# Grouping the eight PV tiles of a step by row half, in a fused attention and gated-MLP kernel

**The chip, the cores and the metric.** The kernel runs on one core of a Trainium2 chip. The metric is the device time of one execution in microseconds (us), as the median of several. All runs of the kernel before and of the change were of the fast state. A single run of a kernel has no state; where only one was made, the text says so.

## The reference, cut to what matters

`x` is 2048 tokens of 576 features. One branch is causal attention with a window of 256 and 32 heads of 18 features, the other a gated MLP; the output joins the two.

```python
q, k, v = split_heads(layernorm(x) @ wqkv)           # 32 heads, 18 features each
scores = jnp.einsum("bhqd,bhkd->bhqk", q, k) * (Dh ** -0.5)
scores = jnp.where(causal_window_256, scores, -1e9)
p = _softmax(scores, axis=-1)
o = jnp.einsum("bhqk,bhkd->bhqd", p, v)              # the PV product: the change is here
s = merge_heads(o) @ wo
g = _silu(_B_ref(layernorm(x), w_gate, w_up, w_down))    # 576 -> 4608 -> 576
return x + s * g
```

## The kernel before

Tokens are worked on in four chunks of 512. A scheduler in the program orders all work at build time from estimated durations; the matmuls of attention are set between those of the MLP. A "PV call" multiplies the exponentials of eight heads (`expr`, keys on the partitions) with their values (`v_aug`, 18 features and a column of ones, so 19 columns). It is a sequence of steps, one per block of 64 keys. In each step the program uses TensorE as eight tiles of 64 rows and 32 columns: two row halves (`i`), for the two halves of the partitions, by four column positions (`g`, `t`). Each tile loads its own 64x19 weights and streams its own columns, which are the queries that can see this block of keys: 64 to 320 of them.

```python
PV_ORDER = (0, 5, -4, -3, -2, -1, 1, 2, 3, 4, 6, 7)
...
ROWS = (slice(0, 64), slice(64, 128))
...
        kss = [ks for ks in PV_ORDER if c or ks >= 0]
        span = {ks: (max(ks, 0), min(ks + 5, SPC)) for ks in kss}

        def f_pv(eng):
            res = None
            outs = self.halves(hp, NT)
            for n, ks in enumerate(kss):
                q0, q1 = span[ks]
                cols = slice(q0 * SW, q1 * SW)
                for g, (hg, where, _) in enumerate(pend):
                    se = where[(ks, q0)]
                    ...
                    for t in range(2):
                        o = sub_pos(c, ks) * VSZ + (2 * hg + t) * VH
                        p0 = 32 * (2 * g + t)
                        for i in range(2):
                            res = eng.matmul(outs[i][p0:p0 + VH, cols], self.v_aug[ROWS[i], o:o + VH],
                                             self.expr[ROWS[i], se, t, cols], start=n == 0, stop=n == len(kss) - 1,
                                             tile_position=(64 * i, p0), skip_group_check=True)
            return res
```

`outs[0]` and `outs[1]` are two neighbouring blocks of 512 columns of the PSUM tensor `ps`, one for each row half. The first chunk has no keys before it, so its four calls have 8 steps (64 matmuls); the other twelve calls have 12 (96 matmuls), of 320, 192, 64, 128, 192, 256, 320, 320, 320, 256, 128 and 64 columns.

Of the kernel before, what the change touches and what calls it, by code (L numbers as in the profile page):

```python
# [32 lines left out]
VH = DH + 1  # L33
VSZ = (H // 2) * VH
# [58 lines left out]
def mm_ns(n):  # L93
    return max(24.7, n / 2.4 + 2.7)
# [9 lines left out]
def unit_slot(c, u):  # L104
    if u < 0:
        return 2 if c % 2 == 0 else 1
    return 0 if u == 0 else (1 if c % 2 == 0 else 2)


def sub_pos(c, ks):  # L110
    return unit_slot(c, ks // 4) * 4 + ks % 4
# [21 lines left out]
def dve_ns(n, rate=1.0):  # L133
    return n / (0.96 * rate) + 160.0
# [114 lines left out]
class Builder:  # L249
# [17 lines left out]
    def op(self, eng, est, fn, name="", deps=(), prio=3, nbytes=0, odeps=(), acq=None):  # L267
        o = Op(eng, est, fn, name, deps, prio, nbytes, odeps, acq)
        o.cidx = len(self.ops)
        self.ops.append(o)  # L270
        for d in o.deps:
            d.succs.append(o)
        for d in o.odeps:
            d.succs.append(o)
        return o
# [502 lines left out]
    def build_pv(self, c, pr):  # L778
        op = self.op
        pend, self.pend = self.pend, []  # L780
        hp = self.pool_s.hold()
        k0 = c * BPC
        vdeps = [self.op_v[kb] for kb in range(max(0, k0 - 2), k0 + BPC)]
# [6 lines that stand above are left out]
            for n, ks in enumerate(kss):  # L790
                q0, q1 = span[ks]
                cols = slice(q0 * SW, q1 * SW)
                for g, (hg, where, _) in enumerate(pend):
                    se = where[(ks, q0)]
                    assert all(where[(ks, q)] == se for q in range(q0, q1))
                    for t in range(2):
                        o = sub_pos(c, ks) * VSZ + (2 * hg + t) * VH
                        p0 = 32 * (2 * g + t)
                        for i in range(2):
                            res = eng.matmul(outs[i][p0:p0 + VH, cols], self.v_aug[ROWS[i], o:o + VH],  # L800
                                             self.expr[ROWS[i], se, t, cols], start=n == 0, stop=n == len(kss) - 1,
                                             tile_position=(64 * i, p0), skip_group_check=True)
            return res
        est = TURN_NS + sum(mm_ns((b - a) * SW) for a, b in span.values())
        pv = op("PE", est, f_pv, f"pv:{c}:{pr}", deps=[[m for _, _, rd in pend for m, _ in rd], vdeps], prio=1, acq=hp)
        for hg, _, rd in pend:
            self.op_pv[(c, hg)] = pv
            for se in sorted({se for _, se in rd}):
                self.r_ex.release(se, pv)
        for i in range(2):  # L810
            p1, d1 = self.r_ot1.produce()
            p2, d2 = self.r_o2.produce()
            p3, d3 = self.r_o2T.produce()
            o1 = self.ot1[:, p1, :].rearrange("p (b d) -> p b d", d=32)
            o2 = self.o2[:, p2, :].rearrange("p (b d) -> p b d", d=32)

            def f_t1(e, i=i, p1=p1):
                return e.transpose(self.ot1[:, p1, :], self.halves(hp, NT)[i])  # L818
            t1 = op("DVE", dve_ns(NT), f_t1, f"ot:{c}:{pr}:{i}", deps=[pv, d1], prio=1)
            hp.release(t1)  # L820
            rc = op("DVE", 255, lambda e, o1=o1: e.reciprocal(o1[:, :, DH], o1[:, :, DH]), f"rc:{c}:{pr}:{i}", deps=[t1], prio=1)
            on = op("DVE", dve_ns(NT // 32 * DH), lambda e, o1=o1, o2=o2: e.tensor_tensor(
                o2[:, :, 0:DH], o1[:, :, 0:DH], o1[:, :, DH:VH].broadcast_to([P, NT // 32, DH]), ALU.mult),
                f"on:{c}:{pr}:{i}", deps=[rc, d2, self.op_o2z], prio=1)
            self.r_ot1.release(p1, on)
            t2 = op("DVE", dve_ns(NT), lambda e, p2=p2, p3=p3: e.transpose(self.o2T[:, p3, :], self.o2[:, p2, :]),  # L826
                    f"ot2:{c}:{pr}:{i}", deps=[on, d3], prio=1)
            self.r_o2.release(p2, t2)
            for n, (k, r0, j0, i0, ni) in enumerate(self.o_moves(pr, i)):
                dst = self.oT[r0:r0 + ni, k, :]  # L830
                sr = self.o2T[32 * j0 + i0:32 * j0 + i0 + ni, p3, :]
                o = self.dma(dst, sr, ni * NT * 2, f"dma:o:{c}:{pr}:{i}:{n}", ("o", pr, i), deps=[t2, self.wo_last], prio=1, eng=OENG[i])
                o.slack = 1000.0
                self.r_o2T.release(p3, o)
                self.op_o.setdefault(c, []).append(o)
        if pr == 0:
            self.op_o[c].append(op("DVE", dve_ns(NT, 4.0), lambda e: e.tensor_copy(self.oT[ROWS[1], 0, :], self.oT[ROWS[0], 0, :]), f"odup:{c}",
                                   deps=[self.op_o[c], self.wo_last], prio=1))
# [458 lines left out]
```

## Time and profile before

| | |
|---|---|
| time, median of the first 3 runs | 560.82 us (560.54 to 561.11) |
| span of the profiled run, granted clock | 558.9 us, 1.000 |
| TensorE (PE) busy | 99% of the span |
| PV calls | 16, 1408 matmuls |

The prediction below shows the totals, the chain and the edges of a call. Here are three of the PV groups, by width of the moving operand. The columns are: line, engine, operation, output and inputs, stationary shape and moving shape, count; then busy time in us and the mean ns of one; then the idle time before them.

```profile
L800 PE MATMUL ps<-expr,v_aug 64*19 64x320 bf16 x512 | 14.7, 297 | 0.0
...
L800 PE MATMUL ps<-expr,v_aug 64*19 64x128 bf16 x224 | 7.2, 216 | 0.0
...
L800 PE MATMUL ps<-expr,v_aug 64*19 64x64 bf16 x224 | 6.4, 189 | 0.0
```

The 512 widest matmuls take 297 ns each, which would be 152 us one after another, but they keep TensorE busy for only 14.7 us: about ten of these records, tails included, lie over each other at a time. So the mean duration says little of the cost. It contains a tail (a 64-column matmul has 189 ns, but in the trace the next step follows a 64-column step after 29 ns) that lies under the next matmuls. What costs is the interval from one step to the next.

### The profile page before, as it was taken

To read this page: it belongs to the slowest core of one execution; us is meant where nothing else is said; L and a number is where in the kernel's file an instruction comes from. 1 tells how busy PE (TensorE), PEld (TensorE's weight loads), DVE (VectorE), ACT (ScalarE), POOL (GpSimd) and SP (SyncE) were. 2 spreads that over 40 slices of the span, in tenths; PEclk is the share of its full clock that TensorE was granted. 3 is DMA by queue.
4 is the path that set the end of the run, shared out by engine and by line. 5 is a ranking of instruction groups with operands and counts; after the bars stand their busy time and mean duration, and the time that the engine had idled before them with its cause. 6 is when DMAs were issued, how large, how long until landed. Compare 5 with 4: busy or idle time off the path is not lost.

```text
span 558.9 us, 19273 instructions
## 1 busy us (share of the span) xinstructions
PE 553.0 (99%) x8342; PEld 339.5 (61%) x8342; DVE 333.6 (60%) x797; ACT 274.3 (49%) x383; POOL 210.8 (38%) x360
## 2 busy tenths in 40 slices
PE   8999999999999999999999999999999999999996
PEld 7454444677755545467886555545688754444786
DVE  5477788687568767574558757357567623333033
ACT  4245654443657655645656464565756342323011
POOL 5564456566245444440667534035373200000000
PEclk9999999999999999999999999999999999999999
DMA  8988997831125534435121264244501035551010
GB/s 224 311 239 191 218 270 221 204 51 45 54 71 155 161 110 144 139 112 95 28 62 44 78 196 115 84 134 130 166 24 47 20 110 154 160 171 48 2 45 23
DMA packets 113468, 67.83 MB, mean 121 GB/s; under 512 B 18620, under 2 KB 111516, under 8 KB 113384
## 3 DMA queue, kind: packets, MB, share of 16 engines
q1 hardware_dynamic: 105960, 60.68, 39.8%
q0 software_dynamic: 7424, 5.92, 4.0%
q8 instruction: 66, 1.08, 0.8%
q14 instruction: 18, 0.15, 0.1%
HBM read 55.15 MB, written 2.36 MB: 103 GB/s over the span
## 4 chain that ended last, share of the span: by engine, by line
PE 98%; DVE 1%; DMA 0%; issue 0%; DVEq 0%
PE ps L121 94%; PE ps L800 3%; DMA x<-in_A_x_dram 0%; DVE small L524 0%; DVE small L526 0%; PE ps L598 0%; DVE xnr L540 0%; DVE s_attn L1061 0%; DVE thf L1066 0%; DVE xnr L544 0%; DVE small L528 0%; DVE small L530 0%; DVE xf L1071 0%; DVEq L1226 0%
## 5 line engine op out<-in xcount | busy, mean ns | idle before, releaser
L121 PE MATMUL ps<-xnT,wgs 64*128 64x512 bf16 (+1 forms) x2400 | 282.5, 368 | 0.1
L750 ACT ACTIVATE expr<-ps 128x1024 bf16<-128x1024 f32 (+4 forms) x160 | 154.9, 969 | 77.8 <-PE ps L121 77.2
L121 PEld LDWEIGHTS ps<-xnT,wgs 64*128 64x128 bf16 x2400 | 113.9, 94 | 114.8 <-DVE hT L948 1.6
L121 PE MATMUL ps<-wd_sb,hT 64*128 64x288 bf16 (+2 forms) x2448 | 156.7, 276 | 0.0
L948 DVE SCALAR_TENSOR_TENSOR hT<-tring,ps 128x512 bf16<-128x512 bf16 x144 | 98.3, 683 | 94.5 <-ACT tring L945 93.4
L945 ACT ACTIVATE tring<-ps 128x512 bf16<-128x512 f32 x144 | 86.1, 598 | 129.7 <-PE ps L121 127.5
L121 PEld LDWEIGHTS ps<-wd_sb,hT 64*128 64x128 bf16 x2448 | 112.4, 94 | 28.6
L278 POOL DMA_DIRECT2D qk<-qd x160 | 82.5, 522 | 119.4 <-PE ps L121 109.5
L763 DVE TENSOR_TENSOR expr<-expr,mask 128x128 bf16<-128x128 bf16 (+2 forms) x240 | 63.6, 298 | 62.0 <-ACT expr L750 61.5
L714 POOL TENSOR_SCALAR kx<-kprev,small 128x256 bf16<-128x256 bf16 x64 | 61.4, 969 | 28.1 <-PE ps L121 27.4
L121 PE MATMUL ps<-qk,kx 64*128 64x320 bf16 (+1 forms) x704 | 59.4, 254 | 0.0
L278 POOL DMA_DIRECT2D oT<-o2T x72 | 36.5, 514 | 58.5 <-DVE o2T L826 49.6
L121 PE MATMUL ps<-xnT,wgr 64*128 64x512 bf16 (+1 forms) x300 | 55.9, 367 | 0.0
L121 PEld LDWEIGHTS ps<-qk,kx 64*128 64x128 bf16 x704 | 31.2, 94 | 21.5 <-ACT expr L750 0.5
L121 PE MATMUL ps<-xnT,wqk 64*128 64x512 bf16 x256 | 32.6, 376 | 0.0
L1051 ACT ACTIVATE thf<-ps 128x576 bf16<-128x576 f32 (+3 forms) x22 | 11.4, 519 | 39.7 <-PE ps L121 39.4
L818 DVE STREAM_TRANSPOSE ot<-ps 128x512 f32<-128x512 f32 x32 | 22.4, 700 | 11.6 <-PE ps L800 11.5
L714 DVE TENSOR_SCALAR kx<-qk,small 128x512 bf16<-128x512 bf16 x64 | 22.4, 378 | 4.7 <-PE ps L121 4.1
L121 PEld LDWEIGHTS ps<-xnT,wgr 64*128 64x128 bf16 x300 | 14.9, 94 | 16.5
L826 DVE STREAM_TRANSPOSE o2T<-o 128x512 bf16<-128x512 bf16 x32 | 22.7, 711 | 1.0
L636 DVE CAST qd<-ps 128x1024 bf16<-128x1024 f32 (+1 forms) x20 | 22.1, 1110 | 1.5 <-PE ps L121 1.5
L696 ACT ACTIVATE v_aug<-ps 64x288 bf16<-64x288 f32 x32 | 13.1, 409 | 17.3 <-PE ps L121 16.8
(71 smaller groups left out, 302.1 us busy)
## 6 DMA issues: line engine op xcount, KB each, us to landing
wgs<-in_B_w_gate_dram SPq DMA_DIRECT2D x72, 256.0 KB, 3.3
wgs<-in_B_w_up_dram SPq DMA_DIRECT2D x72, 256.0 KB, 3.7
wd_sb<-in_B_w_down_dram SPq DMA_DIRECT2D x9, 576.0 KB, 6.3
qk<-qd POOLq DMA_DIRECT2D x100, 36.0 KB, 2.7
wgr<-in_B_w_gate_dram SPq DMA_DIRECT2D x36, 64.0 KB, 2.2
wgr<-in_B_w_up_dram SPq DMA_DIRECT2D x36, 64.0 KB, 2.5
xf<-in_A_x_dram SPq DMA_DIRECT2D x16, 144.0 KB, 2.6
out_dram<-xf SPq DMA_DIRECT2D x15, 144.0 KB, 1.8
```

Of the source, the lines that this page charges most:

```text
L121: res = eng.matmul(outs[i], lhs(ROWS[t], i), rhs(ROWS[t], i), start=start, stop=stop, tile_position=(64 * t, 0))
L278: o = self.op(eng, DMA_ISSUE_NS[eng], lambda e: e.dma_start(dst, src), name, deps, prio, nbytes=nbytes)
L636: return eng.tensor_copy(dst, self.both(h, n))
L696: return eng.activation(dst, src, ACTF.Copy)
L714: return e.tensor_scalar(self.kx[:, sx, pos:pos + n_ // SW, t, :], src.rearrange("p (s k) -> p s k", k=SW), self.half[:, t:t + 1], None, A ...
L750: return eng.activation(self.expr[:, se, :, lo * SW:NT], self.both(h, NT)[:, :, lo * SW:NT], ACTF.Exp, scale=SM_SCALE)
L763: return eng.tensor_tensor(e_, e_, m_, ALU.mult)
L800: res = eng.matmul(outs[i][p0:p0 + VH, cols], self.v_aug[ROWS[i], o:o + VH], self.expr[ROWS[i], se, t, cols], start=n == 0, stop=n == len( ...
L818: return e.transpose(self.ot1[:, p1, :], self.halves(hp, NT)[i])
L826: t2 = op("DVE", dve_ns(NT), lambda e, p2=p2, p3=p3: e.transpose(self.o2T[:, p3, :], self.o2[:, p2, :]), f"ot2:{c}:{pr}:{i}", deps=[on, d3 ...
L945: th = op("ACT", act_ns(NT), lambda e: e.activation(self.tring[:, st, :], bank(h, 0), ACTF.Tanh, scale=0.5), f"th:{c}:{ft}", deps=[pg, dt_ ...
L948: mu = op("DVE", dve_ns(NT), lambda e: e.scalar_tensor_tensor(self.hT[:, ft, :], self.tring[:, st, :], 1.0, bank(h, 1), ALU.add, ALU.mult) ...
```

## The change

The intent is to issue the four tiles of the upper row half together and then those of the lower half, where the kernel before alternates between the halves. The loop over `i` moves from the innermost place to the outermost within a step; operands, flags, counts and the order of steps stay.

```diff
-                for g, (hg, where, _) in enumerate(pend):
-                    se = where[(ks, q0)]
-                    assert all(where[(ks, q)] == se for q in range(q0, q1))
-                    for t in range(2):
-                        o = sub_pos(c, ks) * VSZ + (2 * hg + t) * VH
-                        p0 = 32 * (2 * g + t)
-                        for i in range(2):
+                for i in range(2):
+                    for g, (hg, where, _) in enumerate(pend):
+                        se = where[(ks, q0)]
+                        assert all(where[(ks, q)] == se for q in range(q0, q1))
+                        for t in range(2):
+                            o = sub_pos(c, ks) * VSZ + (2 * hg + t) * VH
+                            p0 = 32 * (2 * g + t)
                             res = eng.matmul(outs[i][p0:p0 + VH, cols], self.v_aug[ROWS[i], o:o + VH],
```

Passages are cut from the recorded text, at the marks, since no trace or run here shows what they rest on: one paragraph, two estimates of a call's length in term 1, and what was said in favour of rival (a), except that an alternating order was chosen here. The sum stands without them: 0 for terms 1, 3 and 4, and 0.1 us slower for term 2 (0.3 if neighbours in one half cost 3 ns each, a supposition): 560.82 + 0.1 = 560.9 us. By "streaming interval" understand what the steps of the first chunk show: 56, 83, 109 and 136 ns after 128, 192, 256 and 320 columns, so some 27 ns for every 64 columns. That steps follow "exactly" at it holds for these, not after the first step of a call (141 to 142 ns) nor after the fourth of a long one (76 ns after 128 columns).

> **What bounds the kernel now.** I read the totals and the chain of waits first, since a reordering inside TensorE's program can only matter if TensorE sets the end.
>
> ```profile
> PE 553.0 (99%) x8342; PEld 339.5 (61%) x8342; DVE 333.6 (60%) x797; ACT 274.3 (49%) x383; POOL 210.8 (38%) x360
> ...
> PE 98%; DVE 1%; DMA 0%; issue 0%; DVEq 0%
> PE ps L121 94%; PE ps L800 3%; DMA x<-in_A_x_dram 0%; DVE small L524 0%; DVE small L526 0%; PE ps L598 0%; DVE xnr L540 0%; DVE s_attn L1061 0%; DVE thf L1066 0%; DVE xnr L544 0%; DVE small L528 0%; DVE small L530 0%; DVE xf L1071 0%; DVEq L1226 0%
> ```
>
> The reader is to see that TensorE (PE) is busy 99% of the span and holds 98% of the chain, and that the changed line, L800 (the PV matmuls), has 3% of it: 3% of 558.9 us is some 19 us. Whatever a PV step gains or loses goes into the end almost one to one, but there are only 19 us to work on.
>
> The chain in order of time shows how those 19 us are made up:
>
> ```profile
> 63.72 0.94 PE ps L800 x64
> ...
> 129.41 0.94 PE ps L800 x64
> 130.35 33.52 PE ps L121 x496
> 163.87 1.27 PE ps L800 x90
> ...
> 438.92 1.27 PE ps L800 x89
> ```
>
> There are sixteen PV calls: four of 64 matmuls (first chunk, 8 steps) at 0.94 us, twelve of 96 (12 steps; a few records are merged into the neighbouring piece) at 1.27 us. 4 x 0.94 + 12 x 1.27 = 19.0 us.
>
> Next I ask what sets the time inside one call: the array, or the issue. The view of line L800 and the stretches of the call that starts at 163.80 us (columns: busy time and instructions in flight of the matmuls, then of the weight loads; the clock; the DMA share and rate):
>
> ```profile
> L800 PEld LDWEIGHTS ps<-expr,v_aug x1408: 83/88/90, 63.7 to 439.9; 64*19 64x19 bf16 x176
> L800 PE MATMUL ps<-expr,v_aug x1408: 189/269/303, 63.7 to 440.0; 64*19 64x320 bf16 x64, 64*19 64x128 bf16 x40, 64*19 64x192 bf16 x28, 64*19 64x256 bf16 x28
> ...
> 163.80:163.93 0.13, 0.13 (x8) 0.13 (x16) 1.00 1.01 300
> 163.95:164.02 0.07, 0.07 (x16) 0.07 (x8) 1.00 1.95 476
> ```
>
> The first stretch is the first step (320 columns): all eight tiles are in flight together, four of the upper row half and four of the lower, and sixteen weight loads (this step's and the next's) have been issued in the same 130 ns. In the trace's single records the eight matmuls of this step start at 0, 4, 7, 10, 14, 17, 20 and 24 ns, and the next step starts 142 ns after the first. In the first chunk the steps start at 0, 141, 224, 360, 495, 631, 740 and 796 ns: the intervals after a 320-column step are 136, 135, 136, after 256 columns 109, after 192 columns 83, after 128 columns 56 ns. So eight tiles take the time of one column stream, and the call is bounded by the array's streaming at full clock, not by the order in which tiles are handed over.
>
> The edges of a call:
>
> ```profile
> 163.49 0.38 PE L121 MATMUL ps<-xnT,wgr 64*128 64x512 bf16 x2
> 163.80 1.34 PE L800 MATMUL ps<-expr,v_aug 64*19 64x320 bf16 x96
> 165.07 0.40 PE L121 MATMUL ps<-qk,kx 64*128 64x64 bf16 x6
> ```
>
> By the single records the next work's first weight load starts 117 to 118 ns after the **last** PV matmul's start (64470 + 4 to 64591 in one call, 164953 to 165071 in another), whichever half it needs, and its loads for both halves go out 3 ns apart.
>
> [...]
>
> **The change part by part.** It removes and adds no instruction: 1408 PV matmuls and as many loads before and after, with the same operands, banks, start and stop flags. It moves them: a step's order goes from U0 L0 U1 L1 U2 L2 U3 L3 to U0 U1 U2 U3 L0 L1 L2 L3. Every tile still comes once in eight, so each tile's next matmul still waits for its own previous one a full step earlier. Term by term:
> 1. Streaming: the sum of the steps per tile is 30 x 64 columns = 1920 in the first chunk and 40 x 64 = 2560 later. [...] Order does not enter. Change: 0.
> 2. Spread within a step: 24 ns in the first chunk (3.3 ns per matmul), 55 ns at the end of the longer calls (last step's last matmul at 1154 against 1099 at its sorted start; by then loads and matmuls arrive about every 4.1 ns each, so a pair in 8.3 ns and eight pairs in 66 ns, longer than the 29 or 56 ns of a 64- or 128-column step). This is supply of instructions, the same number in any order. Change: 0, unless two neighbours in one half cost more than two in different halves; if they cost 3 ns more each, six such neighbours a step add 18 ns once per call as a spread that stays, 16 x 18 = 0.3 us.
> 3. The edge to the next work: it waits for the last matmul, which is L3 both before and after. Change: 0. The upper half is done some 3 positions earlier (3 x 8 = 24 ns), but nothing starts half an array earlier in the trace; if it did, 16 x 24 ns = 0.4 us would be gained.
> 4. Other engines: the PV result's semaphore is set by the same last matmul, so the transposes after it start as before; the order of all other work is computed from estimates the change leaves alone.
> Sum: 0, give or take 0.4 us; I lean 0.1 us to slower for term 2.
>
> **The rivals.** (a) Grouping serialises the loads or matmuls of one half[...]. If two of the four loads of 88 ns a step became visible, 176 steps (4 x 8 + 12 x 12) would add 176 x 176 ns = 31 us, 5.5% slower; one visible load per step 15 us, 2.8%. [...] Against it: the alternating order already has a same-half matmul in flight under every load, and steps follow at exactly the streaming interval. I give it 1%. (b) Alternation itself costs, so fewer changes of half (2 a step in place of 8) speed up PV: at most the 30 ns of extra spread in each of the twelve long calls, 0.4 us, since steps already run at the streaming interval. It can't reach 2%, which would be 11 us of 19. (c) The PV time changes but is hidden by a wait: the chain holds TensorE nearly throughout, so nothing would hide it; this only says that a real difference would be seen.
>
> **Range and chances.** 560.82 + 0.1 gives 560.9 us. The runs before lie within 0.3 us of their median; with 0.4 us for terms 2 and 3 either way and a little for another session, the range is 559.9 to 562.0. Two per cent is 11.2 us, more than half of all PV time, so within 2%: 0.985; slower 0.01 for rival (a), faster 0.005.
>
> **What would show it right or wrong.** In the changed profile: PV calls in the chain of 0.94 and 1.27 us again; eight matmuls in flight in a call's first 130 ns; step intervals of 136 ns after 320 columns; the next work 117 ns after the last PV start. Rival (a) would show as step intervals well over 136 ns or fewer than eight tiles in flight; rival (b) as calls shorter by up to 0.03 us; early start of one half as an edge under 100 ns. The prediction fails if a conflict exists between tiles of one half that only their being neighbours in the program brings out.

## The result, and the profile after

| | before | after |
|---|---|---|
| median of 6 runs | 560.92 us (560.54 to 561.15) | 560.88 us (560.45 to 561.7) |
| ratio after to before | | 1.0, 95% interval 0.9987 to 1.0013 |
| span of the profiled run, granted clock | 558.9 us, 1.000 | 559.3 us, 0.998 |

A ratio is the mean time of one kernel's fast runs over that of the other's of the same rounds, so it is not quite the ratio of the medians. The time is the same.

The totals and the PV calls in the chain of the changed kernel:

```profile
PE 552.5 (99%) x8342; PEld 338.6 (61%) x8342; DVE 333.5 (60%) x797; ACT 274.4 (49%) x383; POOL 210.7 (38%) x360
...
64.16 0.94 PE ps L800 x64
...
129.85 0.94 PE ps L800 x64
...
164.31 1.27 PE ps L800 x89
...
439.35 1.27 PE ps L800 x90
```

Every call takes the 0.94 or 1.27 us that it took before. The first PV call starts at 64.16 us, where it started at 63.72: the 0.4 us by which this one profiled span is longer arose before the first instruction that the change touches, and is no effect of it. From the first call's start to the last one's it is 375.19 us (439.35 - 64.16), against 375.20 before (438.92 - 63.72).

The same two stretches of a call as in the prediction (matmuls busy and in flight, weight loads busy and in flight, clock, DMA), and the edges of the call:

```profile
164.24:164.37 0.13, 0.13 (x8) 0.13 (x16) 1.00 1.13 331
164.39:164.46 0.07, 0.07 (x16) 0.07 (x8) 1.00 0.87 256
```

```profile
163.93 0.38 PE L121 MATMUL ps<-xnT,wgr 64*128 64x512 bf16 x2
164.24 1.34 PE L800 MATMUL ps<-expr,v_aug 64*19 64x320 bf16 x96
165.51 0.40 PE L121 MATMUL ps<-qk,kx 64*128 64x64 bf16 x6
```

Again eight matmuls and sixteen loads in the first 130 ns, a busy 1.34 us, and 1.27 us from the call's start to the next work. By the single records, the steps of this call start at 0, 142, 225, 253, 329, 411, 520, 655, 790, 925, 1034 and 1090 ns (a step's first matmul, told by its width). In the kernel before, the call of the same place has 0, 142, 224, 253, 329, 411, 519, 654, 789, 925, 1034 and 1090. Inside a step, starts are shifted by 4 ns at most (all calls, one by one among the matmuls of a width). Nothing was gained and paid back elsewhere: the changed calls are the same.

### The profile page after: what moved, and what is told of

Read it like the earlier page. It is cut to its first block, busy times and chain, and to the rows that moved or that the text cites. A ratio compares the mean times of both kernels' runs of the same rounds, so it can differ in the third digit from the quotient of the medians.

```text
span 559.3 us, 19273 instructions
## 1 busy us (share of the span) xinstructions
PE 552.5 (99%) x8342; PEld 338.6 (61%) x8342; DVE 333.5 (60%) x797; ACT 274.4 (49%) x383; POOL 210.7 (38%) x360
## 4 chain that ended last, share of the span: by engine, by line
PE 98%; DVE 1%; DMA 0%; issue 0%; DVEq 0%
PE ps L121 94%; PE ps L800 3%; DMA x<-in_A_x_dram 0%; DVE small L524 0%; DVE small L526 0%; PE ps L598 0%; DVE xnr L540 0%; DVE s_attn L1061 0%; DVE thf L1066 0%; DVE xnr L544 0%; DVE small L528 0%; DVE small L530 0%; DVE xf L1071 0%; DVEq L1226 0%
## 5 line engine op out<-in xcount | busy, mean ns | idle before, releaser
L696 ACT ACTIVATE v_aug<-ps 64x288 bf16<-64x288 f32 x32 | 13.1, 409 | 17.3 <-PE ps L121 16.8
```

The costliest lines, as they stand in the source:

```text
L696: return eng.activation(dst, src, ACTF.Copy)
```

## The experiments

That a call did not change doesn't say why. The prediction argued that each tile still comes once in eight, so each waits only for a matmul a full step back. That carries a picture of how TensorE hands out work, which is the author's assumption, and the experiments test it. ("Pair" below is a weight load with its matmul; a single record holds shape and time, not the tile, so a matmul is told by its width.) **Theory A**: matmuls start strictly in program order, each waiting for the earlier one on its own tile. Rivals: order is free, or free within limits, because matmuls wait in queues; or neighbours in one half do cost, but something hid it.

For most of the runs the loop nest was rewritten as a list of (step, row half, tile), whose order is the only thing that differs; the scheduler's estimates are untouched. `L` stands for `len(kss)`, and `tiles` holds the four (g, t). All gave a correct result unless told otherwise. The "last start" in the table is the time from the first to the last matmul start of a call, from the single records; it hardly varies between calls of one kind.

| run | last start, short / long call | growth, all 16 calls | time (before on the same chip) |
|---|---|---|---|
| before, and after | 0.820 / 1.154 us | | 560.92, 560.88 us |
| block2 | 0.833 / 1.237 | 1.05 us | 562.02 us (560.91), 1.002, 1.0005 to 1.0035 |
| block4 | 1.046 / 1.347 | 3.2 | 564.01 us (560.91), one run |
| half | 1.319 / 1.915 | 11.1 | 571.85 us (560.91), 1.0194, 1.0179 to 1.0209 |
| reverse | 0.820 / 1.179 | 0.3 | 561.39 us (560.91), 1.0009, 0.9992 to 1.0026 |
| tile2 | 0.850 / 1.286 | 1.7 | 562.42 us (561.0), one run |
| tile6 | 2.408 / 4.402 | 45.3 | 606.16 us (560.84), one run |
| tileall | 4.310 / 6.522 | 78.4 | 639.23 us (560.84), one run |

The growth is 4 x the short calls' growth + 12 x the long calls'. For half: 4 x 0.499 + 12 x 0.761 = 11.1 us, where the time rose by 10.9; for tileall 78.4 us, where it rose by 78.4. So whatever a PV call loses, the end loses: no wait hides it. That settles rival (c) of the prediction.

### Larger groups of one row half: block2, block4, half

```diff
-order = [(n, i, x) for n in range(L) for x in tiles for i in range(2)]            # before
+order = [(n, i, x) for b0 in range(0, L, B) for i in range(2)
+         for n in range(b0, min(b0 + B, L)) for x in tiles]    # B = 2, 4, and L for "half"
```

> Two steps of the upper half, then the same two of the lower (U U L L), each tile now comes again after 4 matmuls, not 8. Theory A (matmuls are issued strictly in order, and each waits only for the one before it on its own tile): working this through with the measured step times, the last matmul of a call starts 0.24 us later in the four short calls and 0.27 us later in the twelve long ones, 4.2 us in all: 565.1 us. Rival B (each half has a queue of its own, so only the order within a half counts): no change, 560.9 us, calls of 0.94 and 1.27 us. Rival C (neighbours in one row half cost a little each): seven eighths of the neighbours are now in one half, the change has six eighths and cost nothing, so under 0.1 us more.

> Four steps of the upper half, then the same four of the lower. Theory A: four steps of one half run one after another while only the first and the last of them overlap the other half; by the same working 0.55 us more per short call and 0.74 us more per long one, 11 us in all: 572 us. Rival B (own queue per half, deep enough): no change. A queue per half of a few entries would make this slow and the two-step run not.

> All steps of the upper half, then all of the lower: the largest grouping by row half. Theory A: the halves overlap in one step only, calls nearly double, by 0.79 us for a short and 1.07 us for a long one, 16.0 us in all: 576.9 us, with four tiles in flight. Rival D (PV time does not count at the end, a wait hides it): calls double but the total stays within 2 us of 560.9.

Theory A asked for 4.2, 11 and 16 us more; measured were 1.1, 3.1 and 10.9. It fell, most plainly on block4: in its records the first four matmuls of the lower half start at 53 to 63 ns, though twelve matmuls of the upper half that stand before them in the program start only at 142 ns and later. So in this call the issue went past twelve matmuls that had yet to start. Two stretches of that call of block4, which starts at 164.878 us, both end before the upper half's second step; first four tiles are in flight, then eight:

```profile
164.89:164.92 0.03, 0.03 (x4) 0.03 (x8) 1.00 1.40 427
164.95:165.01 0.06, 0.06 (x8) 0.06 (x16) 1.00 1.09 325
```

But it did not go past any number: half costs nearly 11 us, so rival B, a queue deep enough for a whole half, fell too. The chain and the first stretches of a long call of the run half:

```profile
165.83 2.03 PE ps L801 x87
167.86 22.82 PE ps L121 x246
```

```profile
165.76:165.89 0.13, 0.13 (x4) 0.10 (x8) 1.00 1.16 358
165.92:165.98 0.06, 0.06 (x8) 0.06 (x4) 1.00 1.05 300
166.53:166.57 0.04, 0.04 (x16) 0.04 (x12) 1.00 0.00 0
```

In the first 130 ns only four tiles are in flight; the lower half does nothing yet. It joins in the third stretch, 0.77 us into the call. By the records the ninth step of the upper half (320 columns) starts at 772 ns, and a second group of 320-column matmuls, which can only be the lower half's first step, starts at 789. At that moment each upper tile has three more steps to come. In the short calls, of eight steps, the fifth upper step starts at 496 ns and the lower half at 514: again three to come.

### Where a tile comes again at once: reverse, tile2

```diff
+order = [(n, i, x) for n in range(L)                                              # reverse
+         for i, x in [(i, x) for i in range(2) for x in tiles][::-1 if n % 2 else 1]]
+order = [(n, i, x) for b0 in range(0, L, 2) for i in range(2) for x in tiles      # tile2
+         for n in (b0, b0 + 1)]
```

> Every second step runs its eight tiles in reverse order (U0..L3, then L3..U0). Every tile still comes once a step and each half's four still stand together, so if only that mattered (rival E) nothing changes: 560.9 us. Theory A says that the distance of a tile's return matters: the last tile of a step comes again at once, and the others are held up behind it, so each step costs the spread of a step more, 24 ns at a spacing of 3.3 ns: 0.16 us per short call, 0.25 us per long one, 3.7 us in all: 564.6 us, up to 567 if the spread is the 55 ns seen late in long calls.

> Two steps of one tile back to back, then the next tile: a tile comes again at once. Theory A: in-order issue stops at each second matmul until the first has streamed, so tiles overlap by ones; calls grow from 0.94 to 3.9 us and from 1.27 to 4.9 us, 56 us in all: 617 us. Rival F (matmuls can pass one that waits for its tile, so any order within the queue is as good): no change, 560.9 us.

Theory A asked for 3.7 and 56 us more; measured were 0.5 (its interval holds no change) and 1.4. In tile2 the program has a tile's 320-column matmul, then its 192-column one, then the next tile's. Yet the first stretch of a long call shows this:

```profile
163.99:164.12 0.13, 0.13 (x8) 0.13 (x16) 1.00 1.06 311
```

All eight tiles are in flight. The records have their eight 320-column matmuls at 0, 7, 14, 20, 27, 34, 40 and 47 ns, and the first 192-column one at 142. All sixteen loads fall in this stretch too, and the 7 ns from one tile to the next are room for two pairs at 3.3 ns each; yet no second matmul started before 142 ns. We read this as the second matmul waiting at its tile while the issue goes on. In the chain the call has 1.40 us, where theory A asked for 4.9:

```profile
164.06 1.40 PE ps L801 x72
```

Rival F was near, but it allows any order within a queue, which half had refuted.

### The depth of the queue: tile6, tileall

What is left is **theory G**: a queue for each tile that holds one running matmul and three waiting; the issue stops only at a full queue. It is a model of ours, read from the start times of these runs; no record shows a queue. It fits half (three steps to come when the lower half starts) and the start of block4's calls (four steps of each upper tile taken at once). But a limit of twelve waiting matmuls per row half, over all four tiles, would fit them as well (rival H). Long runs of steps on one tile tell these apart, and the expectations were written from a small calculation of both.

```diff
+order = [(n, i, x) for b0 in range(0, L, B) for i in range(2) for x in tiles
+         for n in range(b0, min(b0 + B, L))]                   # B = 6, and L for "tileall"
```

> Six steps of one tile back to back, then six of the next tile (in the short calls six, then the two that are left). Strict in-order issue has fallen: in the run with two steps per tile the eight first matmuls start 7 ns apart. Theory G (each tile has a queue of its own: one matmul running and up to three waiting; the issue goes on to the next tile until it meets a full queue): the second tile starts when the first starts its third step, 0.22 us later, and so on; last starts at 2.3 us in short and 4.3 us in long calls, 44 us in all: 605 us. Rival H (the limit is twelve waiting matmuls per row half, whichever tile they are for): the second tile starts some 20 ns after the first; last starts at 1.37 and 1.8 us, 11 us in all: 572 us. Strict order (theory A) would give far more, over 100 us.

> All steps of one tile, then all of the next. Theory G: the second tile starts when the first has three steps left (0.50 us into a short call, 0.77 us into a long one), each further tile as much later; last starts at 4.26 and 6.48 us, 78 us in all: 639 us. Rival H: last starts at 2.1 and 3.1 us, 29 us in all: 590 us.

Theory G's numbers came out: 606.16 us for 605, 639.23 for 639; rival H's 572 and 590 are far off. Short and long last starts were 2.41 and 4.40 us (2.3 and 4.3 expected), and 4.31 and 6.52 (4.26 and 6.48). In the chain, a long call of tile6 and one of tileall, and then stretches of that of tileall:

```profile
170.44 4.52 PE ps L801 x67
178.06 6.64 PE ps L801 x89
```

```profile
177.99:178.12 0.13, 0.13 (x1) 0.10 (x2) 1.00 1.18 363
...
178.75:178.76 0.01, 0.01 (x2) 0.00 (x0) 1.00 0.00 0
178.78:178.89 0.11, 0.11 (x4) 0.09 (x3) 1.00 0.00 0
```

One matmul is in flight at first. By the records the first tile's ninth step starts at 772 ns and the second tile's first at 778; after the ninth of twelve steps three of that tile are still to come. The runs tell depths apart: by an estimate from the trace's step intervals and 3.3 ns a pair, three waiting put tileall's last start in a long call at 6.46 us, two at 7.41 and four at 5.51; measured is 6.52. Whether such a place would hold matmuls or pairs, the records can't tell. Two loads overlap the one matmul: the second, for the same tile, starts 8 ns into the call, while that tile's next matmul starts at 142 ns.

### Does a neighbour in one half cost anything where streaming can't hide it: shortalt, shortgrp

Both stream only 64 columns in every matmul, so that the steps are short (29 ns after a 64-column step in the kernel before) and a call should be bounded by the supply of instructions, that is, by how fast pairs go out. The result is wrong on purpose (relative error 2.07 in both).

```diff
-                cols = slice(q0 * SW, q1 * SW)
+                cols = slice(q0 * SW, (q0 + 1) * SW)     # shortalt: halves alternate; shortgrp: grouped as in the change
```

> Wrong result on purpose: every PV matmul streams 64 columns only, in the alternating order of the kernel before, so that a call is bounded by the supply of instructions and not by streaming. With pairs of load and matmul arriving every 8.3 ns after the first 32 pairs, the last matmul of a long call starts at 0.65 to 0.86 us (1.15 in the kernel before); the chain's PV pieces shrink to 0.75 to 1.0 us. This is the base for the grouped run.

> The same 64-column matmuls, wrong on purpose, in the grouped order of the change. Theory A: the order is free here too, calls within 0.02 us of the alternating ones. Rival C (a neighbour in the same row half costs, but streaming hid it): with 3 ns for each of six neighbours in a step, 12 x 18 ns = 0.2 us more per long call.

One long call of the alternating and the same one of the grouped run, in their chains:

```profile
162.86 0.87 PE ps L801 x96
```

```profile
162.59 0.87 PE ps L801 x96
```

The last starts are 746 to 748 ns in eleven of the twelve long calls of either run, 826 and 820 in the twelfth. One short call of the grouped run took 0.11 us longer than the other three; why is open, and a cost of neighbours would have shown in all. Rival C would have given 0.2 us more in every long call. After the first 32 pairs the 8.3 ns between pairs could still hide a cost that runs beside the supply. The first 32 can't, at 3.3 ns each: in the calls of these two chains their starts agree position by position within 1 ns, and the first eight are at 0, 3, 7, 10, 13, 17, 20 and 23 ns in both. So a neighbour in the same half costs nothing that these records show. Single runs: 555.37 us alternating, 555.09 grouped.

These runs also size the supply, as measured here. The first pairs go out at 3.3 ns each, and the first 32 matmuls have all started by 131 ns; after a gap of some 90 ns the rest start 8.3 ns apart, 66 ns for a step of eight.

### The order of the steps: longfirst, mixed, mixedgrp

The kernel before has a spread of 64 ns at the end of a long call (its last step runs from 1.090 to 1.154 us) where a short call has 24. The prediction and the expectations have 55, because they took the 89th start in order of time, which is a late 128-column matmul. The fifth step of a long call comes 76 ns after the fourth, whose 128 columns need 56. If steps of 64 and 128 columns (29 and 56 ns) outrun a supply that needs 66 ns, their order should matter where that of the tiles does not.

```diff
-PV_ORDER = (0, 5, -4, -3, -2, -1, 1, 2, 3, 4, 6, 7)
+PV_ORDER = (0, 1, 2, 3, -1, 4, -2, 5, -3, 6, -4, 7)     # longfirst
+PV_ORDER = (0, -4, 1, -3, 2, 6, 3, -2, 5, -1, 4, 7)     # mixed; mixedgrp is this with the change
```

> The kernel before, alternating, with the steps of a call in another order (320-column steps first, the 64-column ones last). If the 55 ns spread at the end of a long call and the 20 ns lost at its fourth and fifth step come from the supply of instructions running dry after three short steps, the long steps let the supply run ahead, the last matmul starts some 55 ns earlier (about 1.10 us after the first, spread 24 ns), the pieces of the chain shrink from 1.27 to about 1.21 us, and the total by 12 x 0.055 = 0.7 us to 560.2 us, too little to be sure of in the total. If the spread comes from the array instead, the calls stay at 1.27 us.

This missed: the calls grew from 1.27 to 1.30 us (561.3 us against 561.0; ratio 1.0005, 0.9992 to 1.0019). Long steps did not let the supply run ahead. In the call below, the loads of the last four steps, all short, arrive mostly 8.3 ns apart, with pauses of 24 to 34 ns between, and the last start is 1.179 us.

```profile
163.91 1.30 PE ps L800 x96
```

So the next run kept short steps from following each other.

> The kernel before, alternating, with short steps set singly between long ones (320, 64, 320, 128, 320, 128, 320, 192, 192, 256, 256, 64 columns). If the spread of 55 ns at the end of a long call needs two or more short steps in a row to arise (three in the kernel before, the last four in the run with long steps first, which got longer), then here no step outruns the supply of a pair every 8.3 ns, the last matmul starts at some 1.10 us, the pieces of the chain are 1.21 us, and the total is 0.6 us less, 560.3 us. If the supply stalls after the first 32 pairs whatever the steps, the pieces stay at 1.27 us or more.

> The change (grouped order in a step) together with the step order of the mixed run. If the order within a step is free and the mixed step order is worth some 0.055 us per long call, this gives what the mixed run gave: long pieces of the chain of 1.21 us, 560.2 to 560.4 us, a ratio to before of 0.9985 to 0.9995. If grouping costs anything once the supply no longer runs dry, the pieces are longer than in the mixed run.

The first long call of the mixed run in its chain, then the first two and the last of mixedgrp:

```profile
164.18 1.22 PE ps L800 x95
```

```profile
163.64 1.22 PE ps L800 x96
187.68 1.22 PE ps L800 x96
...
438.11 1.22 PE ps L800 x96
```

All twelve are 1.22 us in both runs (1.21 was expected). The last start is 1.101 us in both, 53 ns earlier than before: the last step starts at 1.074 us, 16 ns earlier, and its spread is 26 to 28 ns, some 37 less. Twelve times 53 ns is 0.64 us. The mixed run took 560.26 us against 560.84 (ratio 0.9985, 0.9969 to 1.0002), mixedgrp 559.90 against 560.73 (0.9984, 0.997 to 0.9997). So by its calls this step order beats both kernels, by a bit over one part in a thousand; in the totals the interval of mixedgrp lies below 1, that of the mixed run doesn't quite, and neither was timed beside the kernel of the change. The grouping of tiles again adds nothing and takes nothing.

What stays open is how the supply refills. In every call of the short-step runs the first 32 pairs went out 3.3 ns apart and the later ones 8.3; no run tests what sets the 32 or either spacing. The same goes for the 0.08 and 0.2 us by which the long calls of block2 and block4 grew: theory G alone gives 0.01 and 0.04. Over all calls it explains some 0.2 of block2's 1.05 us, 0.6 of block4's 3.2 and 0.4 of tile2's 1.7 (estimates from the step intervals and 3.3 ns a pair), and none of reverse's 0.3, so most of the growth of these four is not explained. Our guess is late arrival of the lower half's pairs: in block4's short calls the loads of the lower half's fifth step do arrive 8.3 ns apart, but no run isolates it.

## Why the prediction was right

- **The number.** 560.9 us predicted, 560.88 measured; calls of 0.94 and 1.27 us, eight tiles in flight, the step intervals and the edge of a call came out as listed under what would show it right.
- **Term 1, streaming**, holds for the change: step starts agree within 1 ns. Its two estimates of a call's length are cut. Measured, the first step of a call is followed after 141 to 142 ns, where later steps of 320 columns are after 135 to 136, and in long calls the fifth step comes after 76 ns, where 128 columns took 56 in the short calls. So "bounded by the array's streaming" is not the whole of a long call; the mixed runs won 53 ns of it.
- **Term 2, spread and supply**, holds for the change. Its allowance of 3 ns for a neighbour in the same half, a supposition, is not seen: the last starts of the grouped and alternating short-step runs agree within 2 ns in eleven of twelve long calls. Its reading of the 8.3 ns as supply got support from the mixed runs (last start 53 ns earlier). But "the same number in any order" is true only of the tiles within a step; for the order of steps the supply matters, by 53 ns a call.
- **Term 3, the edge**, holds: 1.27 us from first start to next work in both, with the last matmul at 1.154 us.
- **The reason given for all this was narrower than what the runs show.** The prediction said that each tile comes once in eight and so waits only for its own matmul a full step earlier; that matmuls start in program order (theory A) was the author's assumption, and block4 and tile2 contradict it. A return once in eight is enough for a zero, but isn't needed for one: tile2 breaks it outright and costs 1.4 us, not the 56 that strict order asks for. What fits the runs in its place is theory G: one matmul of a tile running and three waiting (tileall: the second tile starts at 778 ns, the first tile's ninth of twelve steps at 772), while other tiles' matmuls start ahead of those (tile2: seven other tiles at 7 to 47 ns, the program's second matmul at 142). Under that model the change, with each tile once in eight, stays well inside.
- **Rival (a)**, loads exposed by grouping, up to 31 us: refuted, by sixteen loads over eight matmuls in the first 130 ns of a call in both kernels, and equal step starts. **Rival (b)**, alternation itself costing: refuted, by equal calls with 8 and with 2 changes of half a step. The 30 ns of extra spread that it hoped for (40 by widths) did exist, but belonged to the order of steps.
- **A sum.** 3% of 558.9 us is 16.8 us; the 19.0 us counted from the chain are 3.4%, and nothing rests on the difference.

## What to carry to other kernels

With small tiles packed side by side, ask whether every tile always has a matmul ready, not which neighbour it has in the program: orders that keep within about four matmuls per tile cost little or nothing here (0.6% at most, in block4), and orders beyond that left tiles idle (10.9 us in half, 78.4 in tileall). Where steps are short, count pairs against their measured supply (66 ns for eight here) and try short steps set singly between long ones (calls of 1.22 us in place of 1.27 in the mixed runs). Before a change of order is tried, look whether the interval from step to step grows with the columns alone (here by 27 ns for 64 columns, from 56 to 136 ns): where it did, in the short calls, the reordering within a step won nothing (0.94 us in both kernels).
